# Attention tiles moved to other units of the seven-product blocks, keys summed in the last two units, a tiny exp and sigmoid beside each softmax

## The chip, the cores and the metric

One core of one Trainium2 chip runs the whole program in one launch. The metric is device time in microseconds; the kernel before takes 1980.68 us as the median of three runs (1975.47, 1980.68, 1983.75).

## What is computed

Attention with pooled keys and values, then two feed-forward layers, all in float32:

```python
k_p = k.reshape(B, H, Sp, pool, D).mean(axis=3)      # B 8, H 8, S 576, D 64, pool 8, Sp 72
v_p = v.reshape(B, H, Sp, pool, D).mean(axis=3)
scores = scale * np.matmul(q, k_p.transpose(0, 1, 3, 2))
scores = scores - np.max(scores, axis=-1, keepdims=True)
attn = np.exp(scores)
attn = attn / (np.sum(attn, axis=-1, keepdims=True) + 1e-09)
x = np.matmul(attn, v_p)                             # 4608 tokens x 512
x = (sigmoid(x @ w_gate) * (x @ w_val)) @ w_out      # d_ff 1536
h = x @ w_in
out = elu(h) @ w_out2                                # d_ff 2048
```

The weights arrive as float64. Two int32 words are narrowed to a float32, and each float32 operand is split into a high and a low part, so that three matmuls make one product.

## The kernel before, in words

The 4608 tokens are nine blocks of 512, called block 0 to block 8 here. A block has four tiles of 128 tokens, and the first layer has 12 units of 128 hidden columns for the gate and as many for the value.

Blocks 0 and 1 are computed plainly. Blocks 2 to 8 use seven products in place of eight (the loop `for n in range(SQ, NWB)`): block n runs 12 units u = 0 to 11; an even unit is a gate unit, the odd unit after it is the value unit of the same columns. A unit has seven products k = 0 to 6 (`STEPS`: a11, s2, s3, s1, a12, a22, s4), each of six matmuls of 256 columns on TensorE (L1206), and behind each up to two "filler" matmuls of 512 columns of the layer's second product (L667, `filler`). Three PSUM banks called pl hold the products. What an engine does with a product is written in the same loop: ScalarE copies a11 to u2 (L1216), VectorE adds s2 to it (L1221), s3 to give u3 (L1226), and so on; ScalarE takes the sigmoids in gate units (L1231, L1234, L1237), VectorE multiplies in value units (L1243, L1246, L1251), and g, the product of gate and value, is split by ScalarE (copy, L94) and GpSimd (difference, L95). A bank is overwritten two products later, so TensorE waits when its reader is late.

While block n is multiplied, the attention of block n + 1 is done beside it in small steps, and `thin_plan(n + 1)` says after which (unit, product) each step stands: `load_q`, `q_thin` (four transposes, a ScalarE copy), `s_thin` twice (scores of half the heads; maximum and difference on VectorE), `emit_exp`, `emit_sum`, `emit_norm` (ScalarE adds 1e-9, VectorE takes the reciprocal and a side product pl, GpSimd scales p) and `t_thin` twice (transposes of p, then `keep_p`: ScalarE copies the high part pt, VectorE takes the low part). All of these use one PSUM bank in turn (`one_bank`, tag at1). Keys and values are loaded (`load_kv`), summed over eight rows (`pool_k`, `pool_v`, VectorE) and placed; `k_first` and `k_last` transpose the key sums of the next batch into kbd. Before the next block, `weighted` multiplies p by v into banks pl and at1, and `form_x` makes the seven operands of the next block.

A generator called `working` is the background work: it narrows the weights of the second layer. `work()` takes one step of it, and the table `WORK_AT` (in block 8 also `LAST_AT`) says after which products. A row of w_out2 takes six steps: two of narrowing on VectorE with the store of the row before (L305), two more with the load of the next but one (`fetch`, L132), the split (ScalarE, GpSimd) and `magnitude` (ScalarE, L296), which needs the loaded row. There are two raw buffers, so a load waits on SyncE's queue until the store from the same buffer has landed. `FLUSH_AT` places the copies of the block before out of PSUM.

After block 8 comes the second layer, a long stretch of matmuls (L1327, L1373) that the change leaves alone.

Every engine runs its own list in the order in which the code is written; nothing reorders it at run time.

Of the kernel before, what the change touches and what calls it, by code (L numbers as in the profile page):

```python
# [9 lines left out]
F32 = mybir.dt.float32  # L10
F32R = mybir.dt.float32r
I32 = mybir.dt.int32
AF = mybir.ActivationFunctionType
# [11 lines left out]
def fused_kernel(  # L25
# [12 lines left out]
    nc = tc.nc  # L38
# [4 lines left out]
    P = 128  # L43
    POOL = 8
    SP = S // POOL
    HP = H // 2
    KD = DM // P
    C1 = F1 // P
# [6 lines left out]
    NWB = NT // NW  # L55
    TPW = NW // P
    SQ = 2
    HK = H * SP
    NCH = -(-HK // P)
# [353 lines left out]
    def load_q(t, r=None):  # L413
        r = row_tile("rq") if r is None else r
        for o, n, b, s in segs(t * P, P):
            nc.sync.dma_start(
                out=r[o:o + n].rearrange("p (h d) -> p h d", h=H),
                in_=q[b, :, s:s + n, :].rearrange("h p d -> p h d"),
            )
        q_raw[t] = r  # L420
# [19 lines left out]
    def load_kv(nm, b, c):  # L440
        r = row_tile("rkv")
        if nm == "k":
            r = r[:size(c)]
            nc.sync.dma_start(out=r, in_=rows_of(nm, b)[c * P:c * P + size(c), :])
        else:
            nc.sync.dma_start(out=r, in_=v_rows(b, c))
        kv_raw[nm, b, c] = r
# [18 lines left out]
    def pool_k(b, c):  # L466
        r = kv_raw.pop(("k", b, c))
        n = size(c)
        t = at_p.tile([P, 2, D], F32, name="ks", tag="kv", bufs=NCH)
        nc.vector.tensor_reduce(out=t[:n, 0], in_=r.rearrange("p (r d) -> p d r", r=POOL), op=ALU.add, axis=AX.X)  # L470
        nc.scalar.activation(out=t[:n, 1], in_=t[:n, 0], func=AF.Copy)
        k_sum[b, c] = t
# [4 lines left out]
    def emit_k(b):  # L477

        a = two_banks("atk")
        flat = a.rearrange("p a n -> p (a n)")  # L480
        for c in range(NCH):
            t, n = k_sum.pop((b, c)), size(c)
            nc.tensor.transpose(flat[:, c * P:c * P + n], t[:n].rearrange("p e d -> p (e d)"), ident[:n, :n])
        d = diag(b)
        s = flat[:, :HK].rearrange("p (j e k) -> p j e k", j=HP, e=2)
        nc.scalar.activation(out=d[0:D, :, 0, :], in_=s[0:D, :, 0, :], func=AF.Copy)
        nc.vector.tensor_copy(out=d[D:P, :, 1, :], in_=s[D:P, :, 1, :])
# [70 lines left out]
    def emit_exp(p):  # L558
        nc.scalar.activation(out=p, in_=p, func=AF.Exp, scale=SCALE)
# [3 lines left out]
    def emit_sum(t, p):  # L563
        sm = at_p.tile([P, H], F32, name="sm", tag="sm", bufs=2)
        nc.vector.tensor_reduce(out=sm, in_=p.rearrange("p (h k) -> p h k", k=SP), op=ALU.add, axis=AX.X)
        sums[t] = sm
# [149 lines left out]
    def plan(m):  # L716


        early, pre, mid, post = [[[] for _ in range(C1)] for _ in range(4)]
        for i in range(TPW):  # L720
            t = m * TPW + i
            early[Q_AT[i] - 1].append(lambda t=t: load_q(t))
            pre[Q_AT[i]].append(lambda t=t: emit_q(t))
            pre[S_AT[i]].append(lambda t=t: (t, emit_s(t)))
            mid[T_AT[i]].append(lambda t=t: emit_t(t))
        b = m
        at = (0, 0, 0, 1, 1) if m == 1 else (0, 0, 1, 1, 2)
        for c in range(NCH):
            if m > 1:
                early[at[c]].append(lambda c=c: load_kv("k", b, c))  # L730
                early[4 + c].append(lambda c=c: load_kv("v", b, c))
            post[at[c]].append(lambda c=c: pool_k(b, c))
            post[4 + c].append(lambda c=c: pool_v(b, c))
            post[5 + c].append(lambda c=c: place_v(b, c))
            if m == SQ:
                early[(8, 9, 9, 10, 10)[c]].append(lambda c=c: load_kv("k", b + 1, c))
                post[(9, 9, 10, 10, 11)[c]].append(lambda c=c: pool_k(b + 1, c))
        post[at[-1]].append(lambda: emit_k(b))
        if m == SQ:
            post[11].append(lambda: emit_k(b + 1))  # L740
            early[11].append(lambda: load_q((m + 1) * TPW))
        return early, pre, mid, post

    with tc.manual_schedule():
# [256 lines left out]
        def q_thin(t):  # L1001
# [5 lines left out]
            nc.scalar.activation(out=d, in_=a, func=AF.Copy)  # L1007
            q_t[t] = d

        p_new = {}  # L1010

        def s_thin(t, h):
# [12 lines left out]
        def thin_plan(m):  # L1025


            at = {}

            def put(u, k, f, *a):  # L1030
                at.setdefault((u, k), []).append(lambda: f(*a))

            if m >= NWB:
                return at
            for i in range(TPW):
                t, u = m * TPW + i, 1 + 2 * i
                put(u, 0, q_thin, t)
                put(u, 2, s_thin, t, 0)
                put(u, 4, s_thin, t, 1)
                put(u, 5, lambda t=t: emit_exp(p_new[t]))  # L1040
                put(u + 1, 0, lambda t=t: emit_sum(t, p_new[t]))
                put(u + 1, 1, lambda t=t: emit_norm(t, p_new[t]))
                put(u + 1, 4, t_thin, t, 0, HP)
                put(u + 1, 6, t_thin, t, HP, NCH)
                if i:
                    put(u - 1, 2, load_q, t)
            if m + 1 < NWB:
                put(10, 5, load_q, (m + 1) * TPW)
            if m < B:
                for u, k, c in ((2, 1, 0), (3, 1, 1), (4, 1, 2), (5, 1, 3), (6, 1, 4)):  # L1050
                    put(u, k, load_kv, "v", m, c)
                for u, k, c in ((3, 0, 0), (4, 2, 1), (5, 0, 2), (6, 2, 3), (7, 0, 4)):
                    put(u, k, pool_v, m, c)
                    put(u, k + 2, place_v, m, c)
            if m + 1 < B:
                for u, k, c in ((7, 1, 0), (7, 3, 1), (8, 3, 2), (9, 1, 3), (9, 3, 4)):
                    put(u, k, load_kv, "k", m + 1, c)
                for u, k, c in ((8, 2, 0), (9, 0, 1), (9, 2, 2), (10, 0, 3), (10, 4, 4)):
                    put(u, k, pool_k, m + 1, c)
                put(10, 2, k_first, m + 1)  # L1060
                put(10, 6, k_last, m + 1)
            return at


# [7 lines left out]
            ("s1", 1, True), ("a22", 2, True), ("s4", 1, False),  # L1072
        )
        Y_FILL = ((0, 2, 2, 2, 2, 2, 2), (2, 2, 2, 2, 2, 1, 1))
        Y_FIRST = ((7, 1, 1, 2, 1, 2, 0), (1, 1, 1, 0, 0, 0, 0))
        SHAPE_AT = (0, 3)
        WORK_AT = {(1, 0), (2, 2), (9, 4), (9, 6), (10, 1), (11, 0), (11, 2), (11, 4), (11, 5)}
        WORK_AT |= {(u, k) for u in range(2, C1, 2) for k in (3, 5)} | {(u, k) for u in range(1, C1, 2) for k in (1, 3)}
        WORK_AT |= {(u, 4) for u in (2, 4, 6, 8)}
        FLUSH_AT = ((0, 5), (0, 6), (1, 1), (1, 4))  # L1080
        LAST_AT = ((1, 5), ())

        def weight(nm, cc, i, w3):

# [104 lines left out]
        for n in range(SQ, NWB):  # L1189
            extra = thin_plan(n + 1)  # L1190
            if n > SQ:
                prev_acc = acc
            for u in range(C1):
                cc, i = divmod(u, 2)
                w3 = tt.pop((n - SQ) * C1 + u)
# [4 lines left out]
                for k, (nm, b, opens) in enumerate(STEPS if u else FIRST_STEPS):  # L1200
                    src = bank[b][:, LOW]
                    w = weight(nm, cc, i, w3)
                    m = 0
# [292 lines left out]
```

## Time and profile before

| | |
|---|---|
| median of three runs | 1980.68 us |
| the profiled execution | 1979.38 us, of which its span 1977.7 us |
| TensorE matmuls busy | 1803.1 us (91% of the span) |
| VectorE, ScalarE, GpSimd busy | 1111.0, 856.1, 641.7 us |
| mean granted TensorE clock | 0.97 |
| HBM | 174 GB/s over the span |

TensorE is the busy engine, but its share differs by stage: the page's slices show it lowest at the start and at nine tenths or more in the last 40%. The lists of waits say for each engine how long it stood idle and which instruction ended that; an instruction's line number leads to the code above. PE is TensorE's matmuls, PEld its weight loads, DVE VectorE, ACT ScalarE, POOL GpSimd, SP SyncE, whose queue issues nearly all transfers.

### The profile page before, as it was taken

Reading aid. Unit: us, or ns where it says so; the run is one execution under the profiler, and the core shown is the slowest. Engines: PE = TensorE matmul, PEld = TensorE weight load, DVE = VectorE, ACT = ScalarE, POOL = GpSimd, SP = SyncE. Lnnn points to the kernel's source line nnn. Section 1 sums busy time; section 2 is a strip of 40 time slices with the busy share of each in tenths; the row PEclk is TensorE's granted clock in tenths of the full one; section 3 lists DMA queues with packets and bytes.
Section 4 is the critical chain, followed back from the end, with each engine's and each line's share of the span. In section 5 each row is a group of like instructions: output and inputs, shape, how many; then the busy total and the mean of one; then the engine's idle time right before and its main releaser. Section 6 shows DMA issues by size and latency. Waiting matters only on the chain. (4 is left out here: it accounts for less than half of the span.)

```text
span 1977.7 us, 27958 instructions
## 1 busy us (share of the span) xinstructions
PE 1803.1 (91%) x10212; PEld 1581.3 (80%) x10212; DVE 1111.0 (56%) x2064; ACT 856.1 (43%) x1740; POOL 641.7 (32%) x635
## 2 busy tenths in 40 slices
PE   3677998899898889998999899999999999999999
PEld 2466776687787778787888788999999999999997
DVE  6799567566665667666565565434444344433432
ACT  3355244444444435444344334445444454544533
POOL 2345335333333333333333332222222222222222
PEclk8798999899999999999999999999999999999999
DMA  7254345476665765667656786435334343343431
GB/s 201 92 174 153 110 151 174 152 220 205 208 205 192 234 210 189 210 211 228 205 195 203 266 321 260 156 113 189 131 136 156 112 176 112 138 179 130 153 112 51
DMA packets 150905, 346.81 MB, mean 175 GB/s; under 512 B 47728, under 2 KB 79472, under 8 KB 150768
## 3 DMA queue, kind: packets, MB, share of 16 engines
q1 hardware_dynamic: 150768, 345.02, 51.6%
q8 instruction: 81, 1.33, 0.3%
q14 instruction: 56, 0.46, 0.1%
HBM read 287.31 MB, written 57.67 MB: 174 GB/s over the span
## 5 line engine op out<-in xcount | busy, mean ns | idle before, releaser
L1327 PE MATMUL bank<-form,wr 128*128 128x384 f32 x2016 | 411.0, 338 | 1.0 <-DVE u L1360 0.7
L1327 PEld LDWEIGHTS bank<-form,wr 128*128 128x128 f32 x2016 | 366.5, 188 | 29.1 <-DVE u L1360 1.1
L667 PE MATMUL acc<-g,wos 128*128 128x512 f32 x1152 | 362.1, 402 | 1.9 <-DMA wos<-wd 1.1
L1373 PE MATMUL oacc<-w2o,gc 128*128 128x512 f32 x1080 | 288.9, 393 | 0.4 <-POOL gc L95 0.4
L1373 PEld LDWEIGHTS oacc<-w2o,gc 128*128 128x128 f32 x1080 | 199.6, 187 | 30.4 <-POOL gc L95 0.8
L95 POOL TENSOR_TENSOR g<-sg,g 128x512 fp32r<-128x512 f32 x108 | 142.0, 1319 | 243.4 <-ACT g L94 240.3
L667 PEld LDWEIGHTS acc<-g,wos 128*128 128x128 f32 x1152 | 192.1, 192 | 14.1 <-ACT g L94 1.9
L95 POOL TENSOR_TENSOR gc<-ea,gc 128x384 fp32r<-128x384 f32 x96 | 98.1, 1022 | 298.8 <-ACT gc L94 294.6
L95 POOL TENSOR_TENSOR gc<-pair,gc 128x384 fp32r<-128x384 f32 x96 | 98.0, 1021 | 260.1 <-ACT gc L94 238.1
L1206 PEld LDWEIGHTS pl<-s,wg 128*128 128x128 f32 x1008 | 139.7, 191 | 50.7 <-DVE u L1221 39.5
L1206 PE MATMUL pl<-s,wg 128*128 128x256 f32 x1008 | 155.9, 291 | 26.4 <-DVE u L1221 25.6
L94 ACT ACTIVATE g<-sg 128x512 fp32r<-128x512 f32 x108 | 67.9, 628 | 242.4 <-DVE sg L1246 186.3
L1206 PE MATMUL pl<-a,wg 128*128 128x256 f32 x1008 | 152.2, 287 | 6.9 <-ACT u L1216 3.9
L1206 PEld LDWEIGHTS pl<-a,wg 128*128 128x128 f32 x1008 | 142.3, 193 | 19.0 <-ACT r L924 5.0
L642 PE MATMUL gv<-x,wg 128*128 128x512 f32 x576 | 148.3, 412 | 9.6 <-DVE x L95 5.2
L1206 PE MATMUL pl<-s,tt 128*128 128x256 f32 x1008 | 151.6, 287 | 4.6 <-DVE sg L1236 3.2
L1206 PEld LDWEIGHTS pl<-s,tt 128*128 128x128 f32 x1008 | 141.1, 192 | 14.8 <-DVE sg L1236 3.7
L1373 PE MATMUL oacc<-w2p,gc 128*128 128x512 f32 x540 | 143.1, 393 | 0.0
L642 PEld LDWEIGHTS gv<-x,wg 128*128 128x128 f32 x576 | 112.0, 199 | 35.8 <-issue 6.8
L1373 PEld LDWEIGHTS oacc<-w2p,gc 128*128 128x128 f32 x540 | 99.8, 187 | 14.8
L1340 DVE SCALAR_TENSOR_TENSOR ea<-ea,bank 128x384 f32<-128x384 f32 x48 | 26.6, 555 | 117.2 <-ACT ea L1337 117.2
L1336 ACT ACTIVATE ea<-bank 128x384 f32<-128x384 f32 x48 | 23.6, 492 | 157.5 <-PE bank L1327 157.5
(201 smaller groups left out, 2900.6 us busy)
## 6 DMA issues: line engine op xcount, KB each, us to landing
wr<-wd SPq DMA_DIRECT2D x96, 896.0 KB, 4.9
tt<-td SPq DMA_DIRECT2D x84, 768.0 KB, 4.7
wos<-wd SPq DMA_DIRECT2D x96, 512.0 KB, 5.6
rw<-in_moe_w_out_dram SPq DMA_DIRECT2D x22, 512.0 KB, 4.3
r<-yd SPq DMA_DIRECT2D x24, 384.0 KB, 7.9
out_dram<-po SPq DMA_DIRECT2D x36, 256.0 KB, 2.0
rw<-in_moe_w_in_dram SPq DMA_DIRECT2D x16, 512.0 KB, 4.0
wd<-rw SPq DMA_DIRECT2D x16, 512.0 KB, 5.8
```

What stands on the lines that cost most here:

```text
L94: nc.scalar.activation(out=dst_hi, in_=src, func=AF.Copy)
L95: eng.tensor_tensor(out=dst_lo, in0=src, in1=f32(dst_hi), op=ALU.subtract)
L642: nc.tensor.matmul(d, lhsT=w[:, i, a_w, j], rhs=x[j][:, a_x], start=(j == 0 and a_w == 0 and a_x == 0), stop=(j == KD - 1 and a_w == 1),)
L667: return lambda: nc.tensor.matmul(acc[m], lhsT=w[:, a_w, m * P:(m + 1) * P], rhs=g[:, a_g], start=(c == 0 and a_w == 0 and a_g == 0), stop ...
L1206: nc.tensor.matmul(src, lhsT=w(a_w, j), rhs=f_t[nm][:, j, a_x], start=opens and m == 0, stop=m == 5, skip_group_check=True,)
L1327: nc.tensor.matmul(bank[b ^ flip], lhsT=wp[q][a_w][:, w, j * P:(j + 1) * P], rhs=form_tile(s, a)[j][:, a_x], start=opens and n == 0, stop= ...
L1336: nc.scalar.activation(out=e, in_=src, func=AF.Relu, scale=-1.0)
L1340: nc.vector.scalar_tensor_tensor(out=e, in0=e, scalar=-1.0, in1=src, op0=ALU.add, op1=ALU.max)
L1373: return lambda: nc.tensor.matmul(acc[t + i], lhsT=g[c][:, a_g, i * P:(i + 1) * P], rhs=wo2[2 * q + e][a_w], start=opens and p == 0, stop= ...
```

## The change

In `thin_plan` tile i (i = 0 to 3) moves. Before, its steps start in the odd unit 1 + 2i: queries transposed after product 0, scores after 2 and 4, exp after 5; in the gate unit that follows sum and norm after products 0 and 1, the transposes of p after 4 and 6. Now its queries are transposed in gate unit 2 + 2i after product 4, scores follow after product 6 and after product 1 of the value unit, exp after 2, sum and norm after 3, and p is transposed in the next gate unit, 4 + 2i, after products 0 and 2. Two activations on a 128x1 tile called idle are new for each tile: an exp just before the second scores' exp, a sigmoid just behind it.

The keys of the next batch are summed in units 10 and 11 instead of 8 to 10, `k_first` follows the last product of unit 11, and `k_last` with the last chunk's sum stands in unit 1 of the next block. For block 2 `k_first` stands ahead of the first product, and the last transposes of block 1 go. Value loads and sums are spread over units 2 to 10. `WORK_AT` has 33 steps a block instead of 35, `LAST_AT` adds 30 in block 8 instead of 12, so block 8 takes 63 steps and not 47. Fillers and flushes of units 0 and 1 move by a product or two.

```diff
--- before.py
+++ after.py
@@ -733,12 +733,10 @@
             post[4 + c].append(lambda c=c: pool_v(b, c))
             post[5 + c].append(lambda c=c: place_v(b, c))
             if m == SQ:
-                early[(8, 9, 9, 10, 10)[c]].append(lambda c=c: load_kv("k", b + 1, c))
-                post[(9, 9, 10, 10, 11)[c]].append(lambda c=c: pool_k(b + 1, c))
+                early[(8, 9, 9, 10, 11)[c]].append(lambda c=c: load_kv("k", b + 1, c))
+                if c < NCH - 1:
+                    post[(9, 9, 10, 10)[c]].append(lambda c=c: pool_k(b + 1, c))
         post[at[-1]].append(lambda: emit_k(b))
-        if m == SQ:
-            post[11].append(lambda: emit_k(b + 1))
-            early[11].append(lambda: load_q((m + 1) * TPW))
         return early, pre, mid, post
 
     with tc.manual_schedule():
@@ -1007,6 +1005,12 @@
             nc.scalar.activation(out=d, in_=a, func=AF.Copy)
             q_t[t] = d
 
+        idle = const.tile([P, 2], F32, name="idle")
+
+        def ready(func):
+            nc.scalar.activation(out=idle[:, 1:2], in_=idle[:, 0:1], func=func)
+
+        nc.gpsimd.memset(idle, 0.0)
         p_new = {}
 
         def s_thin(t, h):
@@ -1033,32 +1037,31 @@
             if m >= NWB:
                 return at
             for i in range(TPW):
-                t, u = m * TPW + i, 1 + 2 * i
-                put(u, 0, q_thin, t)
-                put(u, 2, s_thin, t, 0)
-                put(u, 4, s_thin, t, 1)
-                put(u, 5, lambda t=t: emit_exp(p_new[t]))
-                put(u + 1, 0, lambda t=t: emit_sum(t, p_new[t]))
-                put(u + 1, 1, lambda t=t: emit_norm(t, p_new[t]))
-                put(u + 1, 4, t_thin, t, 0, HP)
-                put(u + 1, 6, t_thin, t, HP, NCH)
-                if i:
-                    put(u - 1, 2, load_q, t)
-            if m + 1 < NWB:
-                put(10, 5, load_q, (m + 1) * TPW)
+                t, u = m * TPW + i, 2 + 2 * i
+                put(u + 2, 0, t_thin, t, 0, HP)
+                put(u + 2, 2, t_thin, t, HP, NCH)
+                put(u, 4, q_thin, t)
+                put(u, 6, s_thin, t, 0)
+                put(u + 1, 1, s_thin, t, 1)
+                put(u + 1, 1, ready, AF.Exp)
+                put(u + 1, 2, lambda t=t: emit_exp(p_new[t]))
+                put(u + 1, 3, ready, AF.Sigmoid)
+                put(u + 1, 3, lambda t=t: emit_norm(t, p_new[t]))
+                put(*((u - 1, 1) if i else (1, 3)), load_q, t)
             if m < B:
-                for u, k, c in ((2, 1, 0), (3, 1, 1), (4, 1, 2), (5, 1, 3), (6, 1, 4)):
+                for u, k, c in ((2, 0, 0), (4, 0, 1), (6, 0, 2), (8, 0, 3), (9, 0, 4)):
                     put(u, k, load_kv, "v", m, c)
-                for u, k, c in ((3, 0, 0), (4, 2, 1), (5, 0, 2), (6, 2, 3), (7, 0, 4)):
+                for u, k, c in ((3, 0, 0), (5, 0, 1), (7, 0, 2), (9, 0, 3), (10, 1, 4)):
                     put(u, k, pool_v, m, c)
                     put(u, k + 2, place_v, m, c)
+                put(1, 0, pool_k, m, NCH - 1)
+                put(1, 3, k_last, m)
             if m + 1 < B:
-                for u, k, c in ((7, 1, 0), (7, 3, 1), (8, 3, 2), (9, 1, 3), (9, 3, 4)):
+                for u, k, c in ((9, 1, 0), (10, 1, 1), (10, 3, 2), (10, 5, 3), (11, 5, 4)):
                     put(u, k, load_kv, "k", m + 1, c)
-                for u, k, c in ((8, 2, 0), (9, 0, 1), (9, 2, 2), (10, 0, 3), (10, 4, 4)):
+                for u, k, c in ((10, 4, 0), (11, 0, 1), (11, 2, 2), (11, 4, 3)):
                     put(u, k, pool_k, m + 1, c)
-                put(10, 2, k_first, m + 1)
-                put(10, 6, k_last, m + 1)
+                put(11, 6, k_first, m + 1)
             return at
 
 
@@ -1072,13 +1075,13 @@
             ("s1", 1, True), ("a22", 2, True), ("s4", 1, False),
         )
         Y_FILL = ((0, 2, 2, 2, 2, 2, 2), (2, 2, 2, 2, 2, 1, 1))
-        Y_FIRST = ((7, 1, 1, 2, 1, 2, 0), (1, 1, 1, 0, 0, 0, 0))
+        Y_FIRST = ((6, 1, 1, 1, 1, 1, 0), (1, 1, 1, 1, 1, 1, 0))
         SHAPE_AT = (0, 3)
-        WORK_AT = {(1, 0), (2, 2), (9, 4), (9, 6), (10, 1), (11, 0), (11, 2), (11, 4), (11, 5)}
-        WORK_AT |= {(u, k) for u in range(2, C1, 2) for k in (3, 5)} | {(u, k) for u in range(1, C1, 2) for k in (1, 3)}
-        WORK_AT |= {(u, 4) for u in (2, 4, 6, 8)}
-        FLUSH_AT = ((0, 5), (0, 6), (1, 1), (1, 4))
-        LAST_AT = ((1, 5), ())
+        WORK_AT = {(u, k) for u in range(2, C1, 2) for k in (1, 3, 4, 5)} | {(u, 2) for u in range(1, C1, 2)}
+        WORK_AT -= {(10, 1), (10, 4), (11, 2)}
+        WORK_AT |= {(1, 1), (1, 4), (1, 6), (3, 4), (5, 4), (7, 4), (9, 4), (9, 6), (11, 1), (11, 3)}
+        FLUSH_AT = ((0, 6), (1, 1), (1, 3), (1, 6))
+        LAST_AT = ((0, 1, 5), (0, 4))
 
         def weight(nm, cc, i, w3):
 
@@ -1190,6 +1193,8 @@
             extra = thin_plan(n + 1)
             if n > SQ:
                 prev_acc = acc
+            else:
+                k_first(n + 1)
             for u in range(C1):
                 cc, i = divmod(u, 2)
                 w3 = tt.pop((n - SQ) * C1 + u)
```

On ScalarE, block 4, second tile (before, units 3 and 4; `u` and `pl` are the seven-product tiles, `p` the softmax, `pt` its transpose):

```order
L94 ACTIVATE g<-sg 128x512
L559 ACT_TABLE_LOAD
L559 ACTIVATE p<-p 128x576
L1216 ACTIVATE u_2708<-pl_2705 128x256
L94 ACTIVATE g<-sg 128x512
L573 ACTIVATE sm<-sm 128x8
L494 ACTIVATE vhl<-vs 128x64
L1231 ACT_TABLE_LOAD
L1231 ACTIVATE sg<-pl_2705 128x256
L94 ACTIVATE pt<-att 128x4x128
```

The same tile in the changed kernel, units 5 and 6:

```order
L1221 ACTIVATE u_2695<-pl_2692 128x256
L494 ACTIVATE vhl<-vs 128x64
L1011 ACT_TABLE_LOAD
L1011 ACTIVATE idle<-idle 128x1
L559 ACTIVATE p<-p 128x576
L94 ACTIVATE rs_7116<-nt 128x512
L1011 ACT_TABLE_LOAD
L1011 ACTIVATE idle<-idle 128x1
L573 ACTIVATE sm<-sm 128x8
L94 ACTIVATE g<-sg 128x512
L1221 ACTIVATE u_2695<-pl_2692 128x256
L94 ACTIVATE g<-sg 128x512
```

Exp and its table load stood ahead of the copy of a11 to u2; now they stand behind one such copy, three products ahead of the next. The load for the sigmoid no longer stands ahead of the sigmoid, and the next row of this list is now pt<-att.

On VectorE, block 3, second tile, from the sum of the softmax to the next adds (before):

```order
L1251 TENSOR_TENSOR sg<-sg,u_2708 128x256
L565 TENSOR_REDUCE sm<-p 128x8
L1221 TENSOR_TENSOR u_2708<-u_2708,pl_2706 128x256
L574 RECIPROCAL sm<-sm 128x8
L577 TENSOR_TENSOR pl<-p,sm 128x128
L1226 TENSOR_TENSOR u_2709<-u_2708,pl_2707 128x256
```

The same tile in the changed kernel, through to the next gate unit:

```order
L1245 TENSOR_TENSOR u_2697<-u_2696,pl_2694 128x256
L565 TENSOR_REDUCE sm<-p 128x8
L574 RECIPROCAL sm<-sm 128x8
L577 TENSOR_TENSOR pl<-p,sm 128x128
L1248 TENSOR_TENSOR sg<-sg,pl_2692 128x256
L340 TENSOR_TENSOR nt<-nt 128x256
L341 TENSOR_TENSOR nt<-nt 128x256
L1250 TENSOR_TENSOR u_2696<-u_2696,pl_2693 128x256
L1251 TENSOR_TENSOR sg<-sg,u_2696 128x256
L1255 TENSOR_TENSOR u_2695<-u_2695,pl_2694 128x256
L1256 TENSOR_TENSOR sg<-sg,u_2695 128x256
L95 TENSOR_TENSOR pt<-att,pt 128x4x128
```

The sum stood ahead of the add of s2 (L1221); now sum, reciprocal and pl stand ahead of the multiplication L1248, which reads the bank of a12, and the low part of pt stands ahead of the next add of s2 (L1226 of the changed kernel).

On SyncE's queue in block 8 (rw is the fetched row of w_out2, wod its stored parts, tt the weights of one unit), before, three units:

```order
L885 DMA tt<-td_88 128x1536
L684 DMA wos_10639<-wd_98 128x1024
L1162 DMA wr_10655<-wd_108 128x1792
L1162 DMA wr_10656<-wd_108 128x1792
L1181 DMA w2p<-wod_116 128x1024
L885 DMA tt<-td_89 128x1536
L305 DMA wod_126<-rw_10512 128x1024
L684 DMA wos_10724<-wd_99 128x1024
L132 DMA rw_10747<-in_moe_w_out_dram 128x1024
L1181 DMA w2p<-wod_117 128x1024
L885 DMA tt<-td_90 128x1536
```

The same three units in the changed kernel:

```order
L883 DMA tt<-td_88 128x1536
L684 DMA wos_10683<-wd_98 128x1024
L1165 DMA wr_10701<-wd_108 128x1792
L1165 DMA wr_10702<-wd_108 128x1792
L305 DMA wod_125<-rw_10564 128x1024
L1184 DMA w2p<-wod_116 128x1024
L132 DMA rw_10748<-in_moe_w_out_dram 128x1024
L883 DMA tt<-td_89 128x1536
L684 DMA wos_10773<-wd_99 128x1024
L305 DMA wod_126<-rw_10659 128x1024
L1184 DMA w2p<-wod_117 128x1024
L132 DMA rw_10830<-in_moe_w_out_dram 128x1024
```

Between two loads of tt there is now a store and a fetch in each unit, where one pair served two units.

## Rows read from the trace of the kernel before

**Rows 1.** Busy time by stretch: blocks 2 to 7, block 8, second layer.

```profile
core 0: us, PE busy (x) PEld busy (x) DVE busy (x) ACT busy (x) POOL busy (x), PEclk, DMA share, GB/s
358.40:1103.80 745.40, 675.28 (x4603) 591.89 (x4603) 468.74 (x996) 317.04 (x661) 261.74 (x265) 0.98 0.64 207
1103.80:1209.60 105.80, 96.97 (x640) 88.13 (x641) 67.25 (x137) 35.49 (x79) 32.47 (x29) 0.97 0.79 290
1209.60:1977.70 768.10, 762.96 (x3771) 685.51 (x3769) 314.97 (x567) 355.04 (x719) 198.73 (x194) 1.00 0.39 141
```

**Rows 2.** TensorE matmuls' waits in blocks 2 to 7 (total us, times, longest us).

```profile
PE pl L1206 <- DVE u L1221: 20.8, 27, 1.2
PE atq L1006 <- DVE pt L95: 16.9, 18, 1.9
PE att L587 <- DVE pt L95: 11.2, 16, 1.8
```

**Rows 3.** TensorE weight loads' waits in blocks 2 to 7.

```profile
PEld pl L1206 <- DVE u L1221: 33.4, 29, 1.6
PEld atq L1006 <- DVE pt L95: 24.7, 18, 2.3
PEld att L587 <- DVE pt L95: 19.7, 24, 2.2
```

**Rows 4.** Timeline around the first exp of block 3 (start us, us, engine).

```profile
503.85 0.63 ACT L94 ACTIVATE g<-sg 128x512 fp32r<-128x512 f32 x1 [5.72 <-DVE sg L1246]
504.50 1.28 ACT L559 ACT_TABLE_LOAD   x1
...
505.80 0.69 ACT L559 ACTIVATE p<-p 128x576 f32<-128x576 f32 x1
506.39 0.36 ACT L1216 ACTIVATE u<-pl 128x256 f32<-128x256 f32 x1
506.51 0.75 DVE L565 TENSOR_REDUCE sm<-p 128x8 f32<-128x576 f32 x1 [1.90 <-ACT p L559]
...
507.18 0.41 DVE L1221 TENSOR_TENSOR u<-u,pl 128x256 f32<-128x256 f32 x1
...
507.65 0.98 PE L1206 MATMUL pl<-s,wg 128*128 128x256 f32 x6 [1.20 <-DVE u L1221]
```

**Rows 5.** Groups of instructions in blocks 2 to 7 (busy us, mean ns, idle before).

```profile
L580 POOL TENSOR_TENSOR p<-p,sm 128x576 f32<-128x576 f32 x24 | 27.7, 1153 | 5.4 <-DVE pl L577 4.7 <-DMA tt<-td 0.2 <-DMA rkv<-in_v_dram 0.2
L577 DVE TENSOR_TENSOR pl<-p,sm 128x128 f32<-128x128 f32 x24 | 24.0, 998 | 0.8
L94 ACT ACTIVATE pt<-att 128x512 fp32r<-128x512 f32 (+1 forms) x48 | 20.4, 425 | 0.0
L565 DVE TENSOR_REDUCE sm<-p 128x8 f32<-128x576 f32 x24 | 18.1, 753 | 45.1 <-ACT p L559 45.1
L573 ACT ACTIVATE sm<-sm 128x8 f32<-128x8 f32 x24 | 5.0, 208 | 0.7
```

**Rows 6.** TensorE in gate unit 2 of block 3: a product, then the transposes.

```profile
508.92 0.88 PE L1206 MATMUL pl<-a,wg 128*128 128x256 f32 x6
...
510.12 0.60 PE L587 MATMUL att<-ident,p 128*128 128x128 f32 x4
```

**Rows 7.** Timeline at the end of block 3: ScalarE, TensorE.

```profile
608.72 0.66 ACT L296 ACTIVATE nt<-rw 128x512 f32<-128x512 f32 x1 [6.12 <-DMA rw<-in_moe_w_in_dram]
610.29 0.78 PE L608 MATMUL pl<-pt,vbd 128*128 128x256 f32 x3 [4.81 <-DVE u L1250]
```

**Rows 8.** TensorE at the end of block 1.

```profile
347.97 0.36 PE L483 MATMUL atk<-ident,ks 64*128 64x64 f32 x1 [7.03 <-ACT ks L471]
```

**Rows 9.** Timeline early in block 8: SyncE's queue, ScalarE.

```profile
1121.15 0.38 SPq L305 DMA_DIRECT2D wod<-rw  x1
1128.55 0.33 SPq L132 DMA_DIRECT2D rw<-in_moe_w_out_dram  x1
1136.72 0.66 ACT L296 ACTIVATE nt<-rw 128x512 f32<-128x512 f32 x1 [4.75 <-DMA rw<-in_moe_w_out_dram]
```

## Prediction

> **What bounds the kernel now.** I read the busy time by stretch first [rows 1]. In the second layer TensorE is busy for 762.96 of 768.10 us, and the change does not touch it. In blocks 2 to 7, where the moved steps stand, it is busy for 675.28 of 745.40 us, and the mean granted clock is 0.98: 70 us of idle time, and some of the rest at 1.2 GHz instead of 2.4. That stretch holds what there is to win. Block 8 has 9 us idle in 105.80.
>
> The lists of waits say what ends the idle time. For the matmuls three groups stand out [rows 2]: product s1 waits for VectorE's add of s2 to u2 (L1221), 20.8 us; the queries' transposes wait for the low part of pt, 16.9 us; the fifth transpose of p waits for the same, 11.2 us. Together they are 48.9 us in 24 tiles, 2.0 us a tile. The weight loads' waits for the same causes come to 33.4 + 24.7 + 19.7 = 77.8 us [rows 3]: a matmul's modelled end lies behind the moment at which the next could have started, but a weight load may also be pulled ahead, so the loss lies between the two sums.
>
> The timeline shows why [rows 4]. ScalarE finishes a copy of g, loads the exp table for 1.28 us, runs exp for 0.69 us, and only then copies a11 to u2. VectorE waits 1.90 us for exp before it may sum, and the add of s2 stands behind the sum. TensorE stops for 1.20 us. The other two groups have another cause: queries, two scores and two transposes of p follow each other in one PSUM bank with one or two products between them, and in the gate unit the sigmoid's table load stands on ScalarE ahead of the high part of pt.
>
> **The change, part by part.**
>
> *Exp and its load* now stand in the value unit behind the copy to u2 and three products ahead of ScalarE's next work on a product. The number of table loads is the same. The 48 tiny activations are priced like the shortest row on ScalarE, 0.21 us [rows 5]; they lie where ScalarE is idle otherwise, so they cost nothing unless that cover goes. First the row: the load starts 0.02 us after the g copy ends (503.85 + 0.63 to 504.50), and exp starts 1.30 us after the load did [rows 4]. I take 1.30 us a switch. The Trainium skill ("ScalarE: Activation LUTs", section "What ACT_TABLE_LOAD costs") says that a switch takes about 2.66 us, a drain of 1.38 us included; these rows show no such drain. By its figure each tile's switch would be an estimated 1.36 us longer, and the sum would come out as in the third rival below.
>
> *The bank and the transposes.* Queries, scores and transposes now stand two products apart, some 2.4 us, as the start of a product to that of what follows its two fillers takes 510.12 - 508.92 = 1.20 us [rows 6]. All three groups should go: a gain between 48.9 and 77.8 us. I take 58, nearer to the matmuls' own rows.
>
> *What is late next.* In the value unit VectorE now has, behind s1: an add of 0.41 [rows 4], the sum 0.75, ScalarE's small step and the reciprocal at 0.21 each, pl 1.00 [rows 5], and the multiplication L1248, 0.41: 3.0 us. TensorE has a12, a22 and s4 to do, 3.1 to 3.6 us, before it needs that bank. So it just fits. GpSimd's scaling of p, 1.15 us [rows 5], ends about when the transposes come. Then VectorE does four more adds (1.64 us), ScalarE copies u2, g and pt (0.36, 0.63 and 0.43 us [rows 4, 5]), VectorE takes the low part and adds s2 (about 0.9 us): 6.0 + 0.9 = 6.9 us behind the end of s1. TensorE needs that add in the gate unit at s1, after the three products, a11 without fillers, the transposes and two more products: also 6.9 us. With a background step of VectorE in between, as two thirds of them are, and a handover at each change of engine, it is late by some 0.85 us. For 24 tiles that is 20 us given back; the bounds are 0 and the old 2.0 us a tile, 48 us. I take 20, since the sums meet and only the step and the handovers are over.
>
> *The ends of blocks.* In block 3 a background step makes ScalarE wait 6.12 us for a loaded row, and TensorE stops for 4.81 us [rows 7]. Counted through the code, load and `magnitude` stood three to five products apart eight times in blocks 2 to 7; now it is three times. So -5 us for block 3, and for the three near pairs that stay +4 (0 to 4.8 each). `k_first` behind unit 11 puts copies of about 0.4 us, two on each engine, between the transposes and the part of `weighted` that needs the same bank: 0.7 us in each of five blocks, +3.5 (0 to 8).
>
> *Block 2.* The 7.03 us that TensorE waited for the last key sum [rows 8] go, but `weighted` needs a bank that VectorE reads late there, and four transposes now wait for `form_x` ahead of the first product. I count this as nothing (-3 to +3).
>
> *The clock.* 0.98 on average over 745 us is up to 15 us lost [rows 1]. With fewer stops I take 6 back (0 to 15).
>
> *Block 8.* Here 63 background steps instead of 47. A row needs a store and a load one after the other on SyncE's queue: 1128.55 - 1121.15 = 7.4 us and 1136.72 - 1128.55 = 8.2 us [rows 9], then four narrowing steps about a product apart, 4.8 us. With two buffers a row takes 10.2 us. Six steps at ten in two units of 7.9 us (six times 1.20 and one product without fillers) come every 9.5 us. So each of some nine rows pushes 0.7 us, and ScalarE, which waits 4.75 us in such a step [rows 9], holds the sigmoids behind it; loads of tt queue behind the fetch. I take +7 (0 to 22).
>
> Sum: -58 + 20 - 5 + 4 + 3.5 - 6 + 7 = -34.5 us against the profiled execution of 1979.38 us (span 1977.7 us): **1945 us**. That execution is 1.3 us under the median of the three runs, which is less than they differ among themselves.
>
> **The rivals.**
>
> 1. *The wait only moves.* ScalarE's three copies and a background step hold pt and the add of s2 by as much as before, 2.0 us a tile. For: VectorE's list has the low part of pt ahead of that add, and the background steps crowd into gate units. Against: no table load stands there any more. 1945 + 28 = 1973 us.
> 2. *Block 8 gives more back.* Each of nine rows pushes 2.5 us, since stores and loads meet at a DMA share of 0.79 already [rows 1], and tt comes late. 22 instead of 7: 1960 us.
> 3. *A switch costs more than its row.* If ScalarE's small step waits for the length of a second table load, 1.28 us [rows 4], then L1248 and the next a11 are late by that in each tile: 24 x 1.28 = 31, so 1976 us. The timeline speaks against it, since nothing stands between a load and its neighbours. The Trainium skill's page named above would make something like this of a switch.
> 4. *Slower: softmax becomes the bound of the value unit.* The sum stands ahead of L1248, which frees the bank of a11. VectorE waited 45.1 us for exp before, 1.9 us a tile [rows 5]. If it still does, and the late chain also leaves rival 1's stop, it is 1945 + 28 + 46 = 2019 us. It decides from the point where exp ends over 0.4 us after the add of s1. Against: exp starts two products earlier than the sum needs it.
>
> That the change doesn't do what it says is excluded for the loads: the built order has them ahead of the tiny activations.
>
> **How the numbers follow.** Forecast 0.60, rivals 0.16, 0.12, 0.04 and 0.08. A measurement here can tell about 0.5%, 9.9 us, from no change. Faster by more is below 1970.8: the forecast, half of rival 1 and rival 2 give 0.80. Within it lie the other half of rival 1, rival 3 and a mild form of rival 4: 0.14. Slower: 0.06. The range: without the 20 us of residue and with the small costs at half it would be 1918; with rival 1 and a little more, 1976. The forecast's own range is 1928 to 1960.
>
> **What would show it.** Right: in blocks 2 to 7 the waits of s1 and of the transposes fall from 48.9 to about 20 us, named L1226 and the low part of pt; no ScalarE table load directly ahead of exp; VectorE's wait for exp well under 45 us; block 8 at 108 to 116 us; the second layer at 768 us. Wrong: a wait of a11 for L1248 in each tile (rival 4), block 8 above 120 us (rival 2), or a clock below 0.98 in the blocks.

## The result and the profile after

The changed kernel takes 1950.50 us (median of 4 runs, 1949.15 to 1950.94), the kernel before 1978.08 us (4 runs beside them). The ratio is 0.9858, with a 95% interval of 0.9829 to 0.9887: about 28 us less, and 5.5 us more than forecast. The profiled execution has a span of 1947.4 us, 30.3 us under that of before.

In the changed kernel the lines below the change have moved: the product stands in L1211 (was L1206), the copy to u2 in L1221 (L1216), the add of s2 in L1226 (L1221). First the busy time by stretch (columns as in [rows 1]): blocks 2 to 7, block 8, second layer.

```profile
363.10:1059.90 696.80, 670.11 (x4605) 596.54 (x4603) 462.41 (x979) 325.69 (x696) 249.25 (x260) 0.99 0.67 219
1059.90:1179.30 119.40, 100.07 (x640) 89.57 (x641) 70.31 (x145) 37.40 (x83) 35.66 (x31) 0.94 0.79 279
1179.30:1947.40 768.10, 763.02 (x3771) 685.56 (x3770) 313.66 (x567) 354.80 (x719) 199.04 (x194) 1.00 0.38 141
```

Against [rows 1], blocks 2 to 7 are 48.6 us shorter, block 8 is 13.6 us longer, block 2 starts 4.7 us later, and the second layer is the same: -48.6 + 13.6 + 4.7 = -30.3. Blocks 2 to 7 lose 43.4 us of TensorE's idle time (70.1 to 26.7) and 5.2 us of its busy time, at a granted clock of 0.99 instead of 0.98. Block 8 gains 10.5 us of idle time and 3.1 us of busy time, at a clock of 0.94 instead of 0.97.

The matmuls' waits in blocks 2 to 7 (total us, times, longest us), to be held against [rows 2]:

```profile
PE att L587 <- DVE pt L95: 13.4, 21, 3.1
PE pl L1211 <- DVE u L1226: 3.5, 8, 1.0
...
PE atv L608 <- ACT g L94: 1.4, 3, 0.7
PE pl L1211 <- DVE sg L1248: 1.1, 1, 1.1
```

48.9 us became 16.9. The queries no longer wait for the low part of pt, and the add of s2 holds TensorE for 3.5 us instead of 20.8. Among the groups of the same stretch, VectorE's sum (L565) has lost its 45.1 us of waiting for exp [rows 5], and pl (L577) takes 297 ns instead of 998:

```profile
L1011 ACT ACT_TABLE_LOAD x48 | 61.6, 1283 | 0.8
...
L565 DVE TENSOR_REDUCE sm<-p 128x8 f32<-128x576 f32 x24 | 17.9, 747 | 0.4 <-ACT p L559 0.4
L577 DVE TENSOR_TENSOR pl<-p,sm 128x128 f32<-128x128 f32 x24 | 7.1, 297 | 0.8
```

One softmax of block 2 as it stands now, in the timeline (start us, us, engine, line, operation):

```profile
392.82 1.28 ACT L1011 ACT_TABLE_LOAD   x1
...
394.12 0.20 ACT L1011 ACTIVATE idle<-idle 128x1 f32<-128x1 f32 x1
...
394.41 0.69 ACT L559 ACTIVATE p<-p 128x576 f32<-128x576 f32 x1
...
395.12 1.28 ACT L1011 ACT_TABLE_LOAD   x1
...
395.75 0.75 DVE L565 TENSOR_REDUCE sm<-p 128x8 f32<-128x576 f32 x1
```

The load lies ahead of exp in ScalarE's free time, and exp is done 0.65 us before VectorE takes the sum. In block 8 it is ScalarE that waits, for a row of `w_out2` that has not yet come. Its waits there, after and (second fence) before:

```profile
ACT nt L296 <- DMA rw<-in_moe_w_out_dram: 31.6, 6, 8.8
```

```profile
ACT nt L296 <- DMA rw<-in_moe_w_out_dram: 8.3, 3, 4.8
```

and what TensorE waits for in block 8 after:

```profile
PE pl L1211 <- DVE u L1226: 10.3, 4, 6.5
PE pl L1211 <- DVE u L1231: 3.6, 1, 3.6
```

### The profile page after: what moved, and what is told of

It is laid out like the page before. It is cut to its first block, busy times and chain, and to the rows that moved or that the text cites. A ratio compares the mean times of both kernels' runs of the same rounds, so it can differ in the third digit from the quotient of the medians.

```text
span 1947.4 us, 27985 instructions
## 1 busy us (share of the span) xinstructions
PE 1801.9 (93%) x10212; PEld 1588.1 (82%) x10212; DVE 1110.7 (57%) x2066; ACT 869.8 (45%) x1789; POOL 636.3 (33%) x636
## 4 chain that ended last, share of the span: by engine, by line
PE 43%; DMA 3%; DVE 3%; ACT 1%; issue 1%; SPq 0%; POOL 0%; ACTq 0%; POOLq 0%; DVEq 0%
PE oacc L1378 20%; PE bank L1332 18%; PE pl L1211 2%; DMA wod<-rw 2%; PE acc L667 1%; DMA rw<-in_moe_w_out_dram 1%; DVE nt L117 0%; ACT L1011 0%; DVE a L912 0%; PE ats L533 0%; DVE xe L916 0%; ACT g L94 0%; SPq L701 0%; DVE pt L95 0%; ACT p L559 0%
## 5 line engine op out<-in xcount | busy, mean ns | idle before, releaser
L667 PE MATMUL acc<-g,wos 128*128 128x512 f32 x1152 | 366.5, 403 | 2.8 <-ACT g L94 1.5
L1211 PEld LDWEIGHTS pl<-s,wg 128*128 128x128 f32 x1008 | 142.3, 191 | 37.9 <-DVE u L1226 18.6
L1211 PE MATMUL pl<-s,wg 128*128 128x256 f32 x1008 | 154.9, 289 | 17.1 <-DVE u L1226 13.8
L1211 PEld LDWEIGHTS pl<-a,wg 128*128 128x128 f32 x1008 | 143.0, 194 | 18.4 <-ACT r L922 4.9
L1211 PE MATMUL pl<-a,wg 128*128 128x256 f32 x1008 | 154.1, 290 | 4.2 <-DVE xe L916 2.5
L1211 PE MATMUL pl<-s,tt 128*128 128x256 f32 x1008 | 151.9, 286 | 1.6 <-DVE u L1250 1.6
L1211 PEld LDWEIGHTS pl<-s,tt 128*128 128x128 f32 x1008 | 139.3, 189 | 12.0 <-DVE u L1250 2.4
```

The lines of the kernel that those rows point to most:

```text
L667: return lambda: nc.tensor.matmul(acc[m], lhsT=w[:, a_w, m * P:(m + 1) * P], rhs=g[:, a_g], start=(c == 0 and a_w == 0 and a_g == 0), stop ...
L1211: nc.tensor.matmul(src, lhsT=w(a_w, j), rhs=f_t[nm][:, j, a_x], start=opens and m == 0, stop=m == 5, skip_group_check=True,)
```

## The experiments

Each run's stretches, from its own trace, with its time (median of 4 runs). The ratio is that to the kernel before as it ran beside it: 1978.1 us beside the change, e1, e2, e3 and e6, 1981.7 beside e4, e7, e8 and e9, and 1982.5 beside e5, e10 and e11. The second layer takes 767.9 to 768.1 us in all of them. Two runs, e9 and e10, have the change's own code in blocks 2 to 7, and these took 2.3 and 2.8 us more than in the change's trace: a difference of some 3 us in that column is noise.

| kernel | block 2 starts | blocks 2-7 | block 8 | us | ratio (interval) |
|---|---|---|---|---|---|
| before | 358.4 | 745.4 | 105.8 | 1978.1 | 1 |
| after | 363.1 | 696.8 | 119.4 | 1950.5 | 0.9858 (0.9829-0.9887) |
| e1_even | 361.9 | 692.1 | 102.8 | 1924.5 | 0.9735 (0.9713-0.9757) |
| e2_no_tiny | 362.7 | 692.8 | 121.2 | 1947.1 | 0.9849 (0.9827-0.9870) |
| e3_only_tiny | 356.9 | 720.2 | 109.2 | 1957.5 | 0.9903 (0.9877-0.9928) |
| e4_old_work | 362.0 | 712.9 | 105.4 | 1950.3 | 0.9849 (0.9833-0.9864) |
| e5_new_work | 358.9 | 748.0 | 121.7 | 2000.8 | 1.0093 (1.0078-1.0108) |
| e6_thin_late | 363.1 | 701.0 | 119.1 | 1954.1 | 0.9884 (0.9862-0.9905) |
| e7_kfirst | 356.5 | 704.9 | 121.5 | 1950.6 | 0.9844 (0.9821-0.9866) |
| e8_combo | 356.3 | 689.7 | 104.0 | 1918.5 | 0.9689 (0.9674-0.9704) |
| e9_last_spread | 361.3 | 699.1 | 119.5 | 1950.4 | 0.9852 (0.9834-0.9870) |
| e10_no_load | 362.6 | 699.6 | 99.7 | 1931.0 | 0.9739 (0.9724-0.9754) |
| e11_gate_free | 361.6 | 701.3 | 122.8 | 1954.9 | 0.9861 (0.9844-0.9877) |

### Block 8: even steps, no clumps, no load

```diff
+        WORK_AT |= {(3, 6), (5, 6), (7, 6)}
-        LAST_AT = ((0, 1, 5), (0, 4))
+        LAST_AT = ((), ())
```

> The change with its background steps spread evenly: three more places (units 3, 5, 7 behind product 6), and no extra places in block 8, so 36 a block everywhere instead of 33 and 63. Theory A, block 8 is long because 63 steps make the store-fetch-magnitude round trip of each row collide: block 8 falls from 119.4 to 104-109 us, blocks 2 to 7 grow by 0 to 4, whole 1936-1943 us. Rival B, block 8 is long through its own loads (weights of the second layer, tt): block 8 stays at 115-120, whole 1948-1955.

Block 8 fell to 102.8 us and the whole to 1924.5, both below theory A's ranges. Blocks 2 to 7 did not grow, they fell by 4.7 us: 18 more steps there cost nothing that shows. ScalarE's wait for a loaded row in block 8 is half as long:

```profile
ACT nt L296 <- DMA rw<-in_moe_w_out_dram: 15.3, 5, 5.8
```

The same steps are only dealt out otherwise. Counted through the code, the background work has 253 of them left at block 2, so with the change's places it ends behind the first product of unit 10 of block 8: 55 of the 63 places there do something, against 43 of the 47 before. (A row's load, `fetch`, stands two steps behind the store from the same buffer, and `magnitude` of that row three steps behind the load.) Two runs say what it is about so many steps.

```diff
-        LAST_AT = ((0, 1, 5), (0, 4))
+        LAST_AT = ((0, 2, 6), (0, 5))
```

> The change with the 30 extra steps of block 8 at places of their own (products 0, 2 and 6 of even units, 0 and 5 of odd ones), so that no two stand behind one product; as many steps as before in block 8. Theory A (count: a row needs a store and a load in turn, 15 us, and six steps come sooner): block 8 stays at 113-120 us, whole 1944-1951. Rival B (clumps: two steps behind one product hold VectorE and ScalarE): block 8 at 104-110, whole 1935-1941.

```diff
             if i < len(loads):
+                if i > 24:
+                    raws[i] = raws[i - 2]
+                    return
                 raws[i] = raw_tile("rw2")
```

> The change, but the last seven rows of w_out2 (all of those fetched in block 8 but one) are not loaded: their steps run on the buffer of the row two before, so those rows' values are left out; stores and all 63 steps of block 8 stay. Theory A, the load behind the store is what 63 steps wait for: ScalarE's 31.6 us of waiting for a loaded row go, block 8 at 102-109 us, whole 1932-1941. Rival B, VectorE's and ScalarE's own work of 63 steps is too much for the block: block 8 at 114-120, whole 1944-1952.

Without two steps behind one product block 8 stays at 119.5 us: it is the count, not the clumps. Without the last seven loads it falls to 99.7 us with all the steps in it, and ScalarE's list there has no wait for a row left; both times lie a little below theory A's ranges. The engines' own work for these steps is not too much; the load behind the store is. The stores in front of those loads stayed in this run, so what a store would cost by itself was not tried.

### The places of the background steps, with either attention

> The change with the background steps' places of before (35 a block and 47 in block 8, crowded at the block's end) and all else of the change. Theory A (the round trip of a row): block 8 falls from 119.4 to 104-111 us since there are 47 steps, and fetch and magnitude stand three to five products apart at block ends again, so blocks 2 to 7 grow from 696.8 to 699-709; whole 1938-1948. Rival B (the moved steps themselves crowd block 8, and the gain of blocks 2 to 7 owes nothing to the background): block 8 at 115-121, blocks 2 to 7 at 695-698, whole 1946-1952.

> The kernel before with only the change's places for the background steps (33 a block, 63 in block 8). Theory A, the places of the steps shift time between blocks and win nothing: block 8 grows from 105.8 to 116-121 us, blocks 2 to 7 fall from 745.4 to 725-738, whole 1972-1986. Rival B, clear of block ends they are worth a gain of their own that block 8 does not eat: blocks 2 to 7 under 722, whole 1955-1970.

Both runs swap `WORK_AT` and `LAST_AT`, and nothing else, between the two kernels. Under the change, the old places give the same time to 0.2 us: block 8 is 14.0 us shorter, blocks 2 to 7 are 16.1 us longer (a little over A's range). The waits name the near pairs of fetch and magnitude, and `k_first` behind them: the two waits of TensorE below are 15.4 us, where the change has 1.4. The first fence is ScalarE in blocks 2 to 7 of e4, the second of the change, the third TensorE in e4:

```profile
ACT nt L296 <- DMA rw<-in_moe_w_in_dram: 15.4, 4, 5.7
```

```profile
ACT nt L296 <- DMA rw<-in_moe_w_in_dram: 4.5, 3, 2.9
```

```profile
PE atv L608 <- DVE kbd L991: 10.4, 3, 7.3
...
PE atv L608 <- ACT g L94: 5.0, 1, 5.0
```

With the old attention, the new places bring none of those 16 us: blocks 2 to 7 are 2.6 us longer, block 8 takes its 15.9 us, and the kernel is slower than before by 0.9%. Both of my theories for e5 fell. Its list of waits shows what became of it: TensorE's stops of 4.8 and 2.9 us at block ends are gone, but the three groups of [rows 2] grew from 48.9 to 54.8 us. They stay wherever the steps stand.

```profile
PE pl L1206 <- DVE u L1221: 25.8, 27, 1.4
PE atq L1006 <- DVE pt L95: 16.6, 16, 1.9
PE att L587 <- DVE pt L95: 12.4, 15, 3.0
```

So the change's 28 us are all in what e4 keeps of it, the places of the attention, of its keys, of the fillers and of the flushes. Under these, the steps' places give 16 us in blocks 2 to 7 and lose 14 in block 8.

### The tiny activations

```diff
-                put(u + 1, 1, ready, AF.Exp)
-                put(u + 1, 3, ready, AF.Sigmoid)
```

> The change without its two tiny activations beside each softmax; everything else stays. Theory A, the places of the table loads carry a good part of the gain: exp and the sigmoid wait for a load each, blocks 2 to 7 grow by 8 to 25 us from 696.8, whole 1958-1975. Rival B, the new places of exp and of the transposes do it by themselves, since exp has three products of room: blocks 2 to 7 at 695-701, whole 1948-1954.

The same `ready` put into the kernel before (exp's at product 4 of the value unit, the sigmoid's at 6):

> The kernel before with only the two tiny activations: exp's behind the second half of the scores (product 4 of the value unit), the sigmoid's one product behind exp. Theory A, the load between the g copy and the copy to u2 was what held s1: the wait named L1221 falls from 20.8 to under 8 us, the other two groups stay near 28, whole 1960-1970. Rival B, exp and the sum hold VectorE at that place without the load too: L1221 keeps 14 or more, whole 1973-1981.

The two overlap. In the kernel before, the tiny activations alone take away 20.6 us. The wait of s1 falls from 20.8 to 11.8 us (not under 8). In the tile at 500 us the sigmoid's load now stands ahead of the copy to u2 (it starts at 499.15 us, the copy at 500.56). Against the theory the two other groups fall as well, and the whole is below its range: before, that load stood ahead of the high part of pt (511.79 us, then the sigmoid at 513.08 and pt at 513.36), and now it doesn't. That this is the cause for the two groups was not tried by itself. Blocks 2 to 7 of e3:

```profile
PE pl L1214 <- DVE u L1229: 11.8, 25, 0.9
PE atq L1006 <- DVE pt L95: 9.4, 13, 1.5
...
PE att L587 <- POOL p L580: 4.7, 24, 0.2
```

Under the new places they bring nothing: 1947.1 us without them, a little below rival B's range, where theory A had a loss of 8 to 25 us in blocks 2 to 7. The timeline of e2 shows why: the table load does not wait for exp's data. It runs in ScalarE's free time while VectorE still works on the scores.

```profile
510.88 1.28 ACT L559 ACT_TABLE_LOAD   x1
...
511.83 0.46 DVE L546 TENSOR_TENSOR p<-ats,mx 128x288 f32<-128x288 f32 x1
...
512.33 0.69 ACT L559 ACTIVATE p<-p 128x576 f32<-128x576 f32 x1 [0.16 <-DVE p L546]
```

The sigmoid's load behaves otherwise: in blocks 2 to 7 of e2 ScalarE is idle for 29.8 us ahead of these 24 loads, until TensorE's product is there.

```profile
L559 ACT ACT_TABLE_LOAD x24 | 30.8, 1283 | 0.4
L1234 ACT ACT_TABLE_LOAD x24 | 30.8, 1283 | 29.9 <-PE pl L1209 29.8
```

What costs is a copy to u2 that stands behind load and exp, as in [rows 4]. Moving the loads alone (e3) takes 9 us from that wait; moving exp (e2), which now stands five products ahead of the next copy to u2, takes nearly all of it (20.8 to 4.1 us).

### The residue at the start of the gate unit

```diff
-                put(u + 2, 2, t_thin, t, HP, NCH)
+                put(u + 2, 3, t_thin, t, HP, NCH)
```

> The change with the fifth transpose of p one product later (behind product 4 of the gate unit instead of product 3). Theory A, the 13.4 us that this transpose still waits for the low part of pt are a matter of one product: under 4 us, no other wait takes their place, whole 1938-1946. Rival B, VectorE is late as a whole there, so the wait moves to the add of s2 or to the sigmoids: sum of the waits the same, whole 1947-1955.

```diff
+        WORK_AT -= {(4, 1), (6, 1), (8, 1)}
+        WORK_AT |= {(3, 6), (5, 6), (7, 6)}
```

> The change with three background steps a block taken from gate units 4, 6 and 8 (product 1, between the high and the low part of pt and the add of s2) to the end of value units 3, 5 and 7 (product 6); 33 a block as before. Theory A, the residue is a background step of VectorE ahead of the low part of pt: its 13.4 us fall under 7, L1226 stays under 5, whole 1940-1946. Rival B, the chain of ScalarE's three copies alone makes it late: 11 to 15 us stay, whole 1947-1953.

(In e6's expectation the products are counted from one: it moves the transpose from k = 2 to k = 3.) In e6 the wait moves, as rival B has it, and grows: the transpose no longer waits, and the add of s2 does.

```profile
PE pl L1211 <- DVE u L1226: 25.1, 31, 3.4
```

After the change it was 3.5 us, so the sum of the two grew from 16.9 to 25.1. In e11 the transpose still waits 12.6 us, as rival B has it, and the whole is a little above B's range. But e11 is no test of a background step in between. By the code, a step behind product 1 of the gate unit comes behind the low part of pt and the add of s2 on VectorE's list, and e11 put three of these ahead of the low part. The timeline of one tile after the change (block 3, units 3 and 4; start us, us, engine, line, operation) shows where the time goes:

```profile
515.66 1.15 POOL L580 TENSOR_TENSOR p<-p,sm 128x576 f32<-128x576 f32 x1 [0.87 <-DVE pl L577]
...
515.76 1.60 DVE L117 SCALAR_TENSOR_TENSOR nt<-rw,nt 128x512 int32<-128x512 int32 x1
...
517.28 0.41 DVE L1250 TENSOR_TENSOR u<-u,pl 128x256 f32<-128x256 f32 x1
...
518.52 0.43 DVE L1256 TENSOR_TENSOR sg<-sg,u 128x256 f32<-128x256 f32 x1
...
519.04 0.39 ACT L1221 ACTIVATE u<-pl 128x256 f32<-128x256 f32 x1 [0.22 <-DVE sg L1256]
...
520.47 0.69 DVE L95 TENSOR_TENSOR pt<-att,pt 128x512 fp32r<-128x512 f32 x1 [1.52 <-ACT pt L94]
...
521.21 0.33 PE L587 MATMUL att<-ident,pl 128*128 128x128 f32 x1 [0.43 <-DVE pt L95]
521.40 0.69 DVE L121 SCALAR_TENSOR_TENSOR nt<-rw,nt 128x512 int32<-128x512 int32 x1
```

ScalarE's copies to u2, g and pt can't start before VectorE's last multiplication of the value unit (L1256), and VectorE then waits idle for pt. So a step of VectorE between that multiplication and the low part of pt costs nothing here. The same tile in e11 has its moved step there:

```profile
517.67 0.68 DVE L121 SCALAR_TENSOR_TENSOR nt<-rw,nt 128x512 int32<-128x512 int32 x1
519.27 0.69 DVE L95 TENSOR_TENSOR pt<-att,pt 128x512 fp32r<-128x512 f32 x1 [0.92 <-ACT pt L94]
```

A step that does cost stands further ahead, behind product 4 of the value unit, between L1248 and L1250: L117 above, which takes 1.60 us there beside GpSimd's scaling of p, and 0.69 us in the median of all blocks. The change and e11 both have one at that place in 17 of the 24 tiles. In the change's trace these 17 hold 11.9 of the 13.4 us, and the 7 others 1.5; in e11 it is 12.4 and 0.2. With the old places (e4) only 5 tiles have such a step, and these hold 7.2 of 9.7 us. With the two long waits below left aside, that is 0.41 us a tile against 0.22 in the change, 0.45 against 0.03 in e11 and 0.49 against 0.13 in e4. This is a comparison of tiles; no run took away just these steps.

Of the 13.4 us of the change, two waits in unit 10 make 5.7; the rest are mostly 0.2 to 0.5 us each. The timeline of the longest:

```profile
457.55 1.47 POOL L95 TENSOR_TENSOR g<-sg,g 128x512 fp32r<-128x512 f32 x1
...
457.79 1.51 DVE L340 TENSOR_TENSOR nt<-nt 128x256 f32<-128x256 f32 x1
...
459.38 0.63 ACT L94 ACTIVATE rs<-nt 128x512 fp32r<-128x512 f32 x1 [2.36 <-DVE nt L340]
...
459.92 0.37 ACT L1221 ACTIVATE u<-pl 128x256 f32<-128x256 f32 x1
...
462.07 0.33 PE L587 MATMUL att<-ident,pl 128*128 128x128 f32 x1 [3.10 <-DVE pt L95]
```

Here a background step holds it on ScalarE too: its copy to rs waits for VectorE and stands ahead of the copies to u2, g and pt.

### Block 2's key sums, and all together

```diff
-            else:
-                k_first(n + 1)
+                    if (n, u, k) == (SQ, 0, 5):
+                        k_first(n + 1)
```

> The change with the four transposes of block 2's key sums behind the sixth product of its unit 0 instead of ahead of the first. Theory A, those transposes wait for the lower forms in VectorE's and GpSimd's hands only through the bank they share with attention: the first product of block 2 starts at 357.5-359.5 us instead of 363.1 and the whole is 1944-1947. Rival B, the forms are needed by the next products of unit 0 anyway: the 5 us come back as waits inside unit 0, whole 1948-1952.

Rival B: the block starts 6.6 us earlier, and blocks 2 to 7 are 8.1 us longer, 4.6 of them in unit 0. Ahead of the first product TensorE waits 5.43 us for `form_x` in the change; in e7 it waits for the copy to u2 in unit 0 instead. First the change, then e7:

```profile
362.41 1.09 PE L983 MATMUL atk<-ident,ks 128*128 128x128 f32 x4 [5.43 <-DVE xe L916]
```

```profile
PE pl L1209 <- ACT u L1219: 4.1, 1, 4.1
```

The last run puts e1, e2 and e7 together.

> Even background steps (36 a block), no tiny activations, and the key transposes of block 2 behind its sixth product, all at once. Theory A, the three are independent: 1924.5 less 0 to 3.4 for the tiny ones and 0 to 5 for the transposes, 1916-1924. Rival B, the tiny activations are needed once the background steps stand in the value units' last products (units 3, 5 and 7): 1926-1935.

1918.5 us, 3.1% below the kernel before: the best version of this study. It is 6 us under e1, and blocks 3 to 7, which the key transposes of block 2 do not touch, hold all of it (574.0 us in e1, 567.7 here). That fits the tiny activations costing a little, not helping: with them these blocks take 575.4 us in the change, 577.8 in e9 and 578.2 in e10, and without them 571.3 in e2.

## Why the prediction was right, and where it was not

**The three groups, -58, and the residue, +20.** The mechanism was right. 48.9 us of waits became 16.9, where the forecast said about 20; they have the names it gave, and no table load on the way of u2 is left. By stretch, blocks 2 to 7 fell by 48.6 us and block 2 started 4.7 later, so -43.9, where the terms other than block 8's come to -41.5. The residue is where the forecast put it: 17 of 24 tiles, about its two thirds, have a background step of VectorE in the chain, and they hold 11.9 of the 13.4 us. (That is a comparison of tiles, not an experiment; e11 moved other steps.) But the transposes wait, not the add of s2 (its 3.5 us lie in other units, and most of them in unit 0), and two waits of 5.7 us together have a copy on ScalarE in the way, which the forecast had not named.

**Exp and its load, 1.30 us a switch, tiny ones at nothing.** 392.82 to 394.12 is again 1.30 us. Rival 3 fell: L1248 makes a product of blocks 2 to 7 wait once, for 1.1 us. The Trainium skill's larger figure ("ScalarE: Activation LUTs", section "What ACT_TABLE_LOAD costs") is not seen here either: the tiny activation starts 0.02 us after its load ends. What I did not see is that the new places make the tiny activations needless (e2).

**Ends of blocks, -5 and +4.** The 4.81 us of block 3 [rows 7] are gone. The three near pairs that stay cost ScalarE 4.5 + 2.6 us of waiting in blocks 2 to 7, where before had 23.1 + 8.1, and TensorE's list has no stop like that of block 3: +4 was about 0, which its bounds held. Smaller waits of before went with it, which the forecast did not count ([rows 7] has the 4.81 us; the third row lies in unit 0 of block 2):

```profile
PE atk L985 <- ACT ks L471: 3.3, 4, 1.8
PE pl L608 <- DVE u L1245: 2.9, 1, 2.9
PE pl L1206 <- ACT u L1216: 3.9, 1, 3.9
```

**`k_first` at block ends, +3.5.** No wait of TensorE is named by its copies, so it cost about 0. With steps crowded around it, it cost 10.4 us (e4).

**Block 2, 0.** The key sum's wait went, 5.43 us for `form_x` came, and e7 shows that they come back in another place. The block starts 4.7 us later, and its unit 0 takes 10.48 us instead of 14.36: +0.9 together.

**The clock, -6.** TensorE's busy time in blocks 2 to 7 fell by 5.2 us.

**Block 8, +7.** This term was mis-sized: it measured 13.6 us, nearly halfway to rival 2's 22, and 119.4 us is above the 108 to 116 that the forecast named. The cause is the one named (e9 and e10 show the load behind the store, not steps or clumps). The step that failed is "each of some nine rows pushes 0.7 us": it is 13.6 / 9 = 1.5 us. Its count was wrong. By the tables of the change, units 2 to 9 of block 8 have seven steps in a gate unit and four in a value unit (five in unit 9), so two units have eleven and not ten. Six steps then come every 8.6 us, each row pushes 10.2 - 8.6 = 1.6 us, and the forecast's own sum would have given some 14 us for nine rows. I had also compared the round trip with the mean distance of the steps. But, counted through the code, fetch and magnitude stand two to four products apart in seven jobs there, and in six of them ScalarE waits for the rest of the load, up to 8.8 us, with u2's copy behind it in the longest. The block's mean granted clock is then 0.94, so more of it runs at 1.2 GHz instead of 2.4 than before (0.97), which I had not counted.

**Rivals 1 and 4.** Neither came: the wait did not move as a whole, and the sum waits 0.4 us for exp, not 45.

The sum missed by 4.2 us of span: it took 6.6 us too little for block 8, and 2.4 us too little gain for all else. That the second is so small is luck. The three groups gave 32.0 us of the matmuls' waits, where -58 + 20 stands for 38; all other waits of the matmuls in blocks 2 to 7 fell from 19.3 to 8.6 us (3.9 of that in unit 0 of block 2), where the terms for the ends of blocks come to a loss of 2.5. The two errors have opposite signs.

## What to carry to other kernels

Before forcing a table load to an early place, look whether the function's data come late anyway: exp's load ran by itself in idle time (the sigmoid's did not), and what made it dear was a copy that others wait for, queued behind it. Background work that goes through a store and a load in turn should be spread evenly over everything that can cover it: here 36 steps in each block beat both 35 with 47 at the end and 33 with 63. And when a schedule is changed in two parts, run the two crosswise: here one part was worth all of the gain, and the other was worth nothing, or 1% less than nothing, depending on the first.

## What the runs showed of the hardware that was not expected

pl (L577, 128 columns) took 998 ns before and 1151 ns in e3, but 297 ns after and 348 ns in e2, for the same operation. In the slow cases GpSimd is at work on the lower half of g when it starts; the kernel before:

```profile
507.35 1.28 POOL L95 TENSOR_TENSOR g<-sg,g 128x512 fp32r<-128x512 f32 x1 [1.50 <-ACT g L94]
...
507.78 1.00 DVE L577 TENSOR_TENSOR pl<-p,sm 128x128 f32<-128x128 f32 x1
```

GpSimd's operation ends at 508.63 and VectorE's at 508.78. L340 in the residue's second timeline is another case (256 columns, 1.51 us; GpSimd ends at 459.02, VectorE at 459.30), and L117 in the first (1.60 us; GpSimd ends at 516.81, VectorE at 517.36). VectorE's operation lasts until behind the end of GpSimd's. The Trainium skill ("SBUF — State Buffer", section "SBUF: two separate sides") says that the two share a pair of ports by an exclusive lock, which VectorE needs for two operands from SBUF, and that the later one waits for the whole instruction; these rows agree. So part of VectorE's lateness is paid in operations that look long, not in waits, and pl's 0.7 us a tile came with a change that never meant to touch it.
